# Decode step with sliding attention and a gated layer: the first two loads made one

## The chip, the cores and the metric

The kernel runs on one core of a Trainium2 chip. The metric is the device time of one execution in microseconds. TensorE (PE in the profile, its weight loads PEld), VectorE (DVE), ScalarE (ACT), GpSimd (POOL) and SyncE (SP) run side by side and wait for one another through semaphores. Sixteen DMA engines carry what SyncE issues; every load of this kernel is issued by SyncE.

## The reference

One token of two sequences (`B = 2`, `D = 512`) goes through a layer norm, and then through an attention over the last 2048 places of a cache and a gated layer, whose results are added to the input:

```python
xn = _layernorm(x, axis=-1)
return x + _A_ref(xn, A_k_cache, A_v_cache, A_wq, A_wo) + _B_ref(xn, B_w_gate, B_w_up, B_w_down)

# attention, 32 heads of 128
q = (x @ wq).reshape(B, Sq, Hq, Dh).transpose(0, 2, 1, 3)
k = k_cache[:, :, Sk - W:, :]; v = v_cache[:, :, Sk - W:, :]      # W = 2048
scores = einsum("bhqd,bhkd->bhqk", q, k) * (Dh ** -0.5)
o = einsum("bhqk,bhkd->bhqd", softmax(scores), v)
return o.transpose(0, 2, 1, 3).reshape(B, Sq, Hq * Dh) @ wo

# gated layer, F = 1376
return ((x @ w_gate) * (x @ w_up)) @ w_down
```

All is float32. The keys, values and weights are read once, some 159 MB.

## The kernel before

**One stream in order of use.** The host lays out the keys, values and weights of all heads as one long array, `stream`. The function `blocks()` lists what follows what: blocks, each a list of fields (kind, number, columns). A block is one DMA: 128 rows, one for each partition, and each row is contiguous in memory. A key block of a head is 4096 columns (two sequences, 16 places in each partition, 128 numbers), a value block as much; a quarter of the query weights (`wq`) or of the output weights (`wo`) for a head is 512.

**Tiles and the pump.** A step tile has 13,824 columns (55,296 bytes in each partition), and there are three (`BUFS = 3`). `pump()` walks through the blocks, takes a step tile when a new step begins, and issues the load on SyncE; it stops when three step tiles are held. `done(kind, i)` is called when the program has issued the last reader of a field; with the last field of a tile, the tile is given back and `pump()` goes on. On the chip the load into a reused tile then waits, on SyncE's queue, until the readers of the old contents are through. SyncE issues strictly in this order.

The very first block has a tile of its own, `first`, which is never given back: the input `x` as 8 columns, three small matrices of ones and zeros (`pick`, 16 columns; `rows`, 6; `carry`, 9), and the first quarter of the query weights of head group 0 (`w` 0, 512 columns). Together 551 columns, 275.5 KB. The first step tile then takes `w` 1 (1536 columns), and the keys with `wq` of heads 0 and 1, 5376 KB. The second has the first half of gate and up weights and head 2's keys (6400 KB); the third, the second half, head 3's keys, head 0's values and some of the down weights (6720 KB). From there each step takes three units of key or value, 6912 KB.

**What is done with them.** The layer norm reads `x`: a sum on VectorE, a matmul with a matrix of 1/512 that adds over the partitions, a subtraction, the same again for the squares, a square root on ScalarE, a reciprocal, and a copy that spreads the result to 128 columns (`xnb`). `project_first(0)` multiplies it with `w` 0 to give head 0's query on all partitions, `project_first(1)` with `w` 1 those of heads 1 to 3. For each head VectorE multiplies the keys with the query in place (`products`) and adds up rows of 128 (`sums`); GpSimd takes the maximum over the partitions, ScalarE the exponentials; TensorE weighs the values (`weigh`), `transpose` turns the result with the help of `pick`, and `project_o` adds its product with `wo` to `acc`. Values follow their head's keys by three heads (`LAG`). After head 3's sums comes the gate of the gated layer, whose transposes use `rows`. Near the end `acc` is copied out and goes into a wider form by a matmul with `carry`. The original rows of `x`, in `x_nat`, are added last.

**What sets the order.** TensorE, VectorE, ScalarE and SyncE run their instructions in the order in which the program is written: the wrapper `InOrder` ties each to the one before it, and all their instructions carry its line, L97 in the profile. Tiles are therefore told apart by name.

Of the kernel before, what the change touches and what calls it, by code (L numbers as in the profile page):

```python
# [8 lines left out]
F32 = mybir.dt.float32  # L9
# [7 lines left out]
P = 128  # L17
B, D, H, DH, SK, F = 2, 512, 32, 128, 8192, 1376
W = min(4096, max(256, SK // 4))
J = W // P  # L20
NC = D // P
FB = 4 * P
NFB = -(-F // FB)
# [4 lines left out]
RB = 8  # L28
M = RB * (B - 1) + 1
# [4 lines left out]
CK, CQ, CO = B * J * DH, NC * GC, D  # L34
CP = CQ // NC
UNIT = CK + max(CP, CO)
STEP = 3 * UNIT
# [6 lines left out]
def blocks():  # L44

    def wd(n):
        return [("wd", i, D) for i in range(*WD[n])]

    def k(h):
        return [("k", h, CK)] + ([("wq", h, CP)] if h + HG < H else [])

    def v(h):
        return [("v", h, CK), ("wo", h, CO)]  # L60

    def gu(half):
        n = NC * (FH[half][1] - FH[half][0])
        return [("wg", half, n), ("wu", half, n)]

    units = []
    for h in range(LAG, H - 1):
        units += [k(h), v(h - LAG)]
    ones = [("pick", 0, 8 * B), ("rows", 0, NFB * B), ("carry", 0, M)]
    first = [("x", 0, B * NC)] + ones + [("w", 0, NC * DH)]  # L70
    loads = [[("w", 1, CQ - NC * DH)] + k(0) + k(1), gu(0) + k(2)]
    loads += [gu(1) + units[0] + units[1] + wd(0) + [("wr", 0, NS * P)]]
    loads += [sum(units[i : i + 3], []) for i in range(2, len(units), 3)]
    loads += [k(H - 1) + v(H - 1 - LAG) + wd(1)]
    out = [(("f", 0), first)] + [(("s", i), fields) for i, fields in enumerate(loads)]
    late, last = ("s", len(loads)), ("s", len(loads) + 1)
    out += [(late, v(H - 3)), (late, v(H - 2)), (last, [("v0", H - 1, CL)])]
    out += [(last, [("v1", H - 1, CK - CL)]), (last, [("wo", H - 1, CO)] + wd(2))]
    return out + [(last, wd(n)) for n in range(3, len(WD))]
# [33 lines left out]
def kernel(  # L113
    ctx: ExitStack,
    tc: tile.TileContext,
    x_rows: bass.AP,
    stream: bass.AP,
    out: bass.AP,
):
    nc = tc.nc  # L120
    pe, dve, act, sp = (InOrder(tc, e) for e in (nc.tensor, nc.vector, nc.scalar, nc.sync))
    SCALE = float(DH) ** -0.5
    BUFS = 3

    const = ctx.enter_context(tc.tile_pool(name="const", bufs=1))
    steps = ctx.enter_context(tc.tile_pool(name="steps", bufs=BUFS))
# [6 lines left out]
    for key, fields in blocks():  # L133
        todo.append((key, fields, at))
        at += P * sum(w for _, _, w in fields)
    tiles, used, left, got = {}, {}, {}, {}
    held = 0
# [3 lines left out]
    def pump():  # L141
        nonlocal held
        while todo:
            key, fields, at = todo[0]
            if key not in tiles:
                if key[0] == "f":
                    n = sum(w for _, _, w in fields)
                    tiles[key] = const.tile([P, n], F32, name="first")
                elif held == BUFS:
                    return  # L150
                else:
                    held += 1
                    tiles[key] = steps.tile([P, STEP], F32, name="step")
                used[key] = 0
            todo.pop(0)
            c0 = used[key]
            for kind, i, w in fields:
                got[kind, i] = (tiles[key][:, used[key] : used[key] + w], key)
                used[key] += w
            c1 = used[key]  # L160
            src = stream[at : at + P * (c1 - c0)].rearrange("(p i) -> p i", p=P)
            sp.dma_start(tiles[key][:, c0:c1], src)

    def done(kind, i):
        nonlocal held
        _, key = got.pop((kind, i))
        left[key] -= 1
        if left[key] == 0 and key[0] != "f":
            del tiles[key]
            held -= 1  # L170
            pump()

    pump()
    xT = got["x", 0][0].rearrange("p (b c) -> p b c", b=B)
    pick = got["pick", 0][0].rearrange("p (r s b) -> p r s b", s=2, b=B)
    rows, carry = got["rows", 0][0], got["carry", 0][0][:M]

    x_nat = const.tile([P, P], F32, name="x_nat")
    dve.memset(x_nat, 0.0)
    sp.dma_start(x_nat[::RB, :], x_rows)  # L180

    mean_w = const.tile([P, P], F32, name="mean_w")
    dve.memset(mean_w, 1.0 / D)
# [30 lines left out]
        xc, xT, tr[:, 0:B].unsqueeze(2).to_broadcast([P, B, NC]), op=ALU.subtract  # L214
    )
    dve.tensor_tensor(sq, xc, xc, op=ALU.mult)
    dve.tensor_reduce(st[:, 1, :], sq, axis=AX.X, op=ALU.add)
    pe.matmul(tr[:, 8 : 8 + B], mean_w, st[:, 1, :], start=True, stop=True)
    act.activation(st[:, 2, :], tr[:, 8 : 8 + B], AF.Sqrt, bias=eps_t)
# [20 lines left out]
    def project_first(i):  # L240
        w = got["w", i][0].rearrange("p (c n) -> p c n", c=NC)
        if i == 0:
            q = q_first
        else:
            q_ps[0] = ps_q.tile([P, B, GC], F32, name="q")
            q = q_ps[0][:, :, DH:]
        for b in range(B):
            for c in range(NC):
                pe.matmul(
                    q[:, b, :], xnb[:, c * B + b, :], w[:, c, :],  # L250
                    start=(c == 0), stop=(c == NC - 1),
                )
        done("w", i)
# [26 lines left out]
    def sums(h):  # L280
        s_t[h] = small.tile([P, B, J], F32, name="s")
        dve.tensor_reduce(s_t[h], k_of(h), axis=AX.X, op=ALU.add)
        done("k", h)
# [164 lines left out]
    for _, fields in blocks():  # L448
        ks = [i for kind, i, _ in fields if kind == "k"]
        vs = [i for kind, i, _ in fields if kind == "v"]  # L450
        if vs and vs[-1] >= H - 5:
            break
        for n, h in enumerate(ks):
            products(h)
            project_q(h)
            if 2 <= h <= 3:
                project_gu(h - 2)
            sums(h)
            if h == LAG:
                gate()  # L460
            if vs and n == 0:
                values(vs)
            if h == LAG:
                down(0)
                down_rest()
            maxima(h)
            weights(h)
            if h >= 1:
                reciprocals(h - 1)
# [52 lines left out]
def laid_out(x):  # L522

    import numpy as np

    a = x["A_x"].reshape(B, D)
    first = {
        kind: np.zeros((P, w), a.dtype) for kind, _, w in blocks()[0][1][:4]
    }
    first["x"][:] = a.reshape(B, P, NC).transpose(1, 0, 2).reshape(P, B * NC)  # L530
    for b in range(B):
        for r in range(4):
            for s in range(2):
                first["pick"][8 * s + 4 * b + r :: 32, (2 * r + s) * B + b] = 1.0
        for n in range(NFB):
            first["rows"][32 * n + b, n * B + b] = 1.0
        first["carry"][RB * b, RB * b] = 1.0
    cache = {
        kind: x[name][:, :, SK - W :, :].reshape(B, H, P, J * DH).transpose(1, 2, 0, 3)
        for kind, name in (("k", "A_k_cache"), ("v", "A_v_cache"))  # L540
    }
    wq = x["A_wq"].reshape(P, NC, H // HG, GC).transpose(2, 0, 1, 3)
    wo = x["A_wo"].reshape(H, P, D)
    gu = {
        kind: x[name].reshape(P, NC, F)
        for kind, name in (("wg", "B_w_gate"), ("wu", "B_w_up"))
    }
    wd = x["B_w_down"]
    rest = wd[NFC * P :].reshape(FR, NS + 1, P)

    def field(kind, i):
        if kind in first:
            return first[kind]
        if kind in ("k", "v"):
            return cache[kind][i].reshape(P, CK)
        if kind in ("v0", "v1"):
            v = cache["v"][i].reshape(P, CK)
            return v[:, CL:] if kind == "v1" else v[:, :CL]
        if kind == "w":
            return (wq[0][:, :, DH:] if i else wq[0][:, :, :DH]).reshape(P, -1)  # L560
        if kind == "wq":
            return wq[i // HG + 1][:, i % HG, :]
        if kind == "wo":
            return wo[i]
        if kind == "wr":
            last = rest[:, NS, :].reshape(NS, FX, P).swapaxes(0, 1)
            return np.concatenate([rest[:, :NS, :], last]).reshape(P, NS * P)
        if kind == "wd":
            return wd[i * P : (i + 1) * P]
        return gu[kind][:, :, FH[i][0] : FH[i][1]].reshape(P, -1)  # L570

    parts = [
        np.concatenate([field(kind, i) for kind, i, _ in fields], axis=1).ravel()
        for _, fields in blocks()
    ]
    x_rows = np.zeros((D // P, 32 // RB, P), a.dtype)
    x_rows[:, :B] = a.reshape(B, D // P, P).transpose(1, 0, 2)
    return {
        "x_rows": x_rows.reshape(-1, P),
        "stream": np.concatenate(parts),  # L580
    }

# [31 lines left out]
```

## Time and profile before

| | |
|---|---|
| runs, median (lowest to highest) | 377.33 us (377.32 to 377.37), 3 runs |
| the profiled execution | 377.5 us |
| its span, first to last instruction | 375.7 us |
| HBM read | 159.48 MB |
| DMA issues on SyncE | 32, of them 30 into `first` and the step tiles |
| TensorE's granted clock, mean | 0.805 |

The span leaves out what lies before the first and after the last instruction, here 1.8 us. In the lines of the profile `step<-in_stream_dram` is a load into a step tile, `first<-in_stream_dram` the load of the first tile; SPq is SyncE's queue of issues. A number in brackets behind a line of the timeline is the idle time of that engine before it, and what ended it. The view of DMA issues gives the time from the issue of a load until its last byte has landed.

### The profile page before, as it was taken

The numbers are of one execution on the slowest core, as the hardware profiler recorded it, in microseconds if no ns is written. First come the engines' busy times: TensorE is split into PE (matmuls) and PEld (weight loads), VectorE is DVE, ScalarE is ACT, GpSimd is POOL, SyncE is SP. The second block draws the span as 40 slices with busy tenths as digits, with TensorE's granted clock in tenths as the row PEclk, the third lists the DMA queues.
The fourth block names the chain that finished last, engine by engine and source line by source line (L and its number), as shares of the span: only waits on it lengthen the run. The fifth ranks groups of instructions, "written<-read, shape, count | busy, mean of one in ns | idle before, by whom it ended". The sixth has DMA issues, their size and how long they took to land.

```text
span 375.7 us, 2858 instructions
## 1 busy us (share of the span) xinstructions
PE 254.2 (68%) x1084; PEld 88.5 (24%) x1084; DVE 294.1 (78%) x146; ACT 58.6 (16%) x259; POOL 25.3 (7%) x78
## 2 busy tenths in 40 slices
PE   3496497886547486854858476685846669637996
PEld 3241023331112122211212121231212122212334
DVE  3299691998599499769949976994996799599950
ACT  1021001122021111201112020211202011211131
POOL 1001000000000000100000100000000000000010
PEclk9998967998697666888768696885869676857999
DMA  8999999899999999999999999999999999999995
GB/s 346 445 436 454 426 408 471 383 465 449 395 466 406 442 455 400 459 418 436 460 400 449 424 430 459 402 442 430 430 459 406 437 444 436 419 431 443 398 421 221
DMA packets 4492, 159.70 MB, mean 425 GB/s; under 512 B 512, under 2 KB 640, under 8 KB 1152
## 3 DMA queue, kind: packets, MB, share of 16 engines
q1 hardware_dynamic: 4480, 159.54, 98.5%
q8 instruction: 8, 0.13, 0.1%
q14 instruction: 4, 0.03, 0.0%
HBM read 159.48 MB, written 0.06 MB: 425 GB/s over the span
## 4 chain that ended last, share of the span: by engine, by line
DMA 63%; DVE 26%; PE 8%; ACT 1%; issue 0%; SPq 0%; DVEq 0%
DMA step<-in_stream_dram 63%; DVE s L97 13%; DVE step L97 13%; PE o_ps L97 3%; PE q L97 2%; PE acc L97 2%; PE tr L97 1%; ACT o_sb L97 0%; DVE m L97 0%; ACT oT L97 0%; SPq L97 0%; DVE rec L97 0%; DVE o_out L97 0%; DVEq L97 0%
## 5 line engine op out<-in xcount | busy, mean ns | idle before, releaser
L97 DVE TENSOR_TENSOR step<-step,q 128x4096 f32<-128x4096 f32 x31 | 136.6, 4407 | 52.4 <-DMA step<-in_stream_dram 52.4
L97 PE MATMUL q<-step,xnb 128*128 128x512 f32 (+1 forms) x128 | 92.4, 872 | 76.4 <-DMA step<-in_stream_dram 76.4
L97 DVE TENSOR_REDUCE s<-step 128x32 f32<-128x4096 f32 x32 | 141.4, 4419 | 1.1
L97 PE MATMUL o_ps<-step,p 128*16 128x512 f32 x512 | 68.9, 672 | 11.5 <-DMA step<-in_stream_dram 11.5
L97 PEld LDWEIGHTS q<-step,xnb 128*128 128x128 f32 x128 | 32.3, 275 | 130.5 <-DMA step<-in_stream_dram 77.5
L97 PE MATMUL acc<-step,oT 128*9 128x512 f32 (+1 forms) x88 | 35.4, 552 | 9.3 <-ACT oT L97 8.1
L97 PE MATMUL tr<-first,o_sb 128*128 128x2 f32 (+2 forms) x198 | 28.1, 261 | 15.4 <-ACT o_sb L97 13.0
L97 ACT COPY o_sb<-o_ps 128x512 f32<-128x512 f32 (+1 forms) x25 | 14.1, 568 | 140.7 <-PE o_ps L97 140.7
L97 PEld LDWEIGHTS tr<-first,o_sb 128*128 128x128 f32 x198 | 26.0, 200 | 36.8 <-ACT o_sb L97 32.4
L290 POOL PARTITION_ALL_REDUCE mm<-m x32 | 11.3, 354 | 283.1 <-DVE rec L97 180.1
L97 PEld LDWEIGHTS o_ps<-step,p 128*16 128x16 f32 x512 | 13.4, 104 | 69.9 <-issue 54.4
L97 ACT ACTIVATE nm<-mm 128x2 f32<-128x2 f32 x32 | 6.5, 203 | 131.4 <-POOL mm L290 131.4
L97 ACT ACTIVATE p<-s,nm 128x16 f32<-128x16 f32 x64 | 19.2, 300 | 1.0
L97 ACT ACTIVATE oT<-tr,rec 128x1 f32<-128x1 f32 x64 | 12.2, 260 | 28.5 <-PE tr L97 28.5
L306 POOL PARTITION_ALL_REDUCE sum<-rs x32 | 12.7, 398 | 55.0 <-ACT p L97 55.0
L97 PE MATMUL o_ps<-step,xn 128*2 128x512 f32 (+1 forms) x48 | 13.9, 616 | 0.0
L97 ACT ACTIVATION_READ_ACCUMULATOR p<-s,nm 128x1 f32 x64 | 12.0, 187 | 0.0
L97 DVE TENSOR_TENSOR step<-step,tr 128x4096 f32<-128x4096 f32 x1 | 4.4, 4422 | 9.3 <-DMA step<-in_stream_dram 9.3
L97 PEld LDWEIGHTS acc<-step,oT 128*9 128x9 f32 x88 | 4.5, 91 | 19.4 <-ACT oT L97 12.7
L97 PE MATMUL q<-xnb,mean_w 128*128 128x512 f32 (+2 forms) x18 | 8.3, 551 | 0.0
L97 DVE TENSOR_TENSOR o_out<-acc,x_nat 128x128 f32<-128x128 f32 x1 | 0.3, 292 | 8.8 <-PE acc L97 8.8
L97 DVE TENSOR_REDUCE m<-s 128x2 f32<-128x32 f32 x32 | 5.9, 186 | 1.1
(39 smaller groups left out, 40.5 us busy)
## 6 DMA issues: line engine op xcount, KB each, us to landing
step<-in_stream_dram SPq DMA_DIRECT2D x16, 6912.0 KB, 31.1
step<-in_stream_dram SPq DMA_DIRECT2D x2, 6400.0 KB, 32.8
step<-in_stream_dram SPq DMA_DIRECT2D x1, 6720.0 KB, 45.4
step<-in_stream_dram SPq DMA_DIRECT2D x1, 6656.0 KB, 29.0
step<-in_stream_dram SPq DMA_DIRECT2D x1, 5376.0 KB, 15.3
step<-in_stream_dram SPq DMA_DIRECT2D x1, 4864.0 KB, 29.6
step<-in_stream_dram SPq DMA_DIRECT2D x2, 2304.0 KB, 17.1
step<-in_stream_dram SPq DMA_DIRECT2D x1, 1536.0 KB, 14.6
```

Source lines behind the costliest of these rows:

```text
L97: made = call(*args, **kwargs)
L290: nc.gpsimd.partition_all_reduce(mm, m, P, bass_isa.ReduceOp.max)
L306: nc.gpsimd.partition_all_reduce(sum_t[h], rs, P, bass_isa.ReduceOp.add)
```

## The change

The first block loses its tile. `x`, `pick` and `rows` become the first fields of the first step tile, followed by all of `w`, and the whole is one load of 11,294 columns (45,176 bytes a row). Since a step tile is given back, `pick` and `rows`, which are needed later, are copied by ScalarE into tiles of their own as soon as the load has landed; `x` is given up after the subtraction. `carry` leaves the stream and becomes an input of its own, 9 x 9, loaded by a DMA that SyncE issues behind that of `x_nat`. The constant tiles become 2048 bytes smaller in each partition, and all later tiles move down by as much. In the program built from it, ScalarE has one more load of its function table, between the two copies and the square root.

```diff
-    ones = [("pick", 0, 8 * B), ("rows", 0, NFB * B), ("carry", 0, M)]
-    first = [("x", 0, B * NC)] + ones + [("w", 0, NC * DH)]
-    loads = [[("w", 1, CQ - NC * DH)] + k(0) + k(1), gu(0) + k(2)]
+    first = [("x", 0, B * NC), ("pick", 0, 8 * B), ("rows", 0, NFB * B)]
+    loads = [first + [("w", 0, NC * DH), ("w", 1, CQ - NC * DH)] + k(0) + k(1), gu(0) + k(2)]
...
-    out = [(("f", 0), first)] + [(("s", i), fields) for i, fields in enumerate(loads)]
+    out = [(("s", i), fields) for i, fields in enumerate(loads)]
...
             if key not in tiles:
-                if key[0] == "f":
-                    n = sum(w for _, _, w in fields)
-                    tiles[key] = const.tile([P, n], F32, name="first")
-                elif held == BUFS:
+                if held == BUFS:
                     return
-                else:
-                    held += 1
-                    tiles[key] = steps.tile([P, STEP], F32, name="step")
+                held += 1
+                tiles[key] = steps.tile([P, STEP], F32, name="step")
...
-        if left[key] == 0 and key[0] != "f":
+        if left[key] == 0:
...
-    pick = got["pick", 0][0].rearrange("p (r s b) -> p r s b", s=2, b=B)
-    rows, carry = got["rows", 0][0], got["carry", 0][0][:M]
+    pick_t = const.tile([P, 8 * B], F32, name="pick")
+    act.copy(pick_t, got["pick", 0][0])
+    done("pick", 0)
+    pick = pick_t.rearrange("p (r s b) -> p r s b", s=2, b=B)
+    rows = const.tile([P, NFB * B], F32, name="rows")
+    act.copy(rows, got["rows", 0][0])
+    done("rows", 0)
...
+    carry = const.tile([M, M], F32, name="carry")
+    sp.dma_start(carry, carry_rows)
...
     dve.tensor_tensor(sq, xc, xc, op=ALU.mult)
+    done("x", 0)
```

The rest of the difference passes the new input through and fills it on the host's side, as before.

More of the change, by code (lines that the diff above doesn't have):

```diff
@@ L116 @@
     x_rows: bass.AP,
+    carry_rows: bass.AP,
     stream: bass.AP,
@@ L527, in laid_out @@
     first = {
-        kind: np.zeros((P, w), a.dtype) for kind, _, w in blocks()[0][1][:4]
+        kind: np.zeros((P, w), a.dtype) for kind, _, w in blocks()[0][1][:3]
     }
+    carry = np.zeros((M, M), a.dtype)
     first["x"][:] = a.reshape(B, P, NC).transpose(1, 0, 2).reshape(P, B * NC)
@@ L536, in laid_out @@
             first["rows"][32 * n + b, n * B + b] = 1.0
-        first["carry"][RB * b, RB * b] = 1.0
+        carry[RB * b, RB * b] = 1.0
     cache = {
@@ L579, in laid_out @@
         "x_rows": x_rows.reshape(-1, P),
+        "carry": carry,
         "stream": np.concatenate(parts),
```

## The prediction

> **What bounds the kernel now.** First the page: the busy shares, the queues, the chain that ended last.
>
> ```profile
> PE 254.2 (68%) x1084; PEld 88.5 (24%) x1084; DVE 294.1 (78%) x146; ACT 58.6 (16%) x259; POOL 25.3 (7%) x78
> ...
> q1 hardware_dynamic: 4480, 159.54, 98.5%
> q8 instruction: 8, 0.13, 0.1%
> ...
> DMA 63%; DVE 26%; PE 8%; ACT 1%; issue 0%; SPq 0%; DVEq 0%
> ```
>
> The DMA engines are busy 98.5% of the span; VectorE, the fullest engine, 78%. The chain puts 26% on VectorE. Read alone, that says that a later VectorE makes a later end. The reader has to check this against the transfers, because the chain stops at the instruction that released a load's issue, whether or not the queue was empty by then. So next: when each load is issued (SyncE's timeline, four windows), and how long it takes to land (the DMA view, the windows at 43 and 72 us).
>
> ```profile
> 0.72 0.38 SPq L97 DMA_DIRECT2D first<-in_stream_dram  x1
> 1.16 1.37 SPq L97 DMA_DIRECT2D step<-in_stream_dram  x3
> 34.54 0.33 SPq L97 DMA_DIRECT2D step<-in_stream_dram  x1
> 43.58 0.33 SPq L97 DMA_DIRECT2D step<-in_stream_dram  x1
> 72.90 0.33 SPq L97 DMA_DIRECT2D step<-in_stream_dram  x1
> ...
> step<-in_stream_dram SPq DMA_DIRECT2D x1, 6912.0 KB, 37.9
> ...
> step<-in_stream_dram SPq DMA_DIRECT2D x1, 6912.0 KB, 24.9
> ```
>
> Call the loads into step tiles s0, s1, s2 (issued one after the other from 1.16 us), s3 (34.54), s4 (43.58), s5 (72.90). s4 lands at 43.58 + 37.9 = 81.5, s5 at 72.90 + 24.9 = 97.8: 16.3 us apart for 6912 KB (7.08 MB), 434 GB/s. s5 was issued 8.6 us before s4 had landed. Who waited for the early landings (timeline), and the chain at both ends of the program:
>
> ```profile
> 16.58 4.42 DVE L97 TENSOR_TENSOR step<-step,tr 128x4096 f32<-128x4096 f32 x1 [9.33 <-DMA step<-in_stream_dram]
> 31.62 2.65 PE L97 MATMUL q<-step,xnb 128*128 128x512 f32 x4 [3.26 <-DMA step<-in_stream_dram]
> 47.48 4.42 DVE L97 TENSOR_TENSOR step<-step,q 128x4096 f32<-128x4096 f32 x1 [3.67 <-DMA step<-in_stream_dram]
> 65.25 4.42 DVE L97 TENSOR_TENSOR step<-step,q 128x4096 f32<-128x4096 f32 x1 [7.16 <-DMA step<-in_stream_dram]
> ...
> 1.16 15.32 DMA step<-in_stream_dram
> ...
> 34.54 30.69 DMA step<-in_stream_dram
> ...
> 343.55 19.66 DMA step<-in_stream_dram
> 363.21 0.04 issue
> ...
> DVE step L97 <- DMA step<-in_stream_dram: 61.7, 11, 9.3
> ```
>
> s0 lands at 16.48, s1 at 31.6, s2 at 47.5, s3 at 65.23. s3, issued at 34.54, had s2 still 12.9 us from landing. In every case the next load stood in the queue before the one ahead was through, and VectorE waited 61.7 us in all for data. The queue sets the end; the chain's VectorE pieces at the front are work that the queue covers. They count only if a load's issue becomes so late that the queue empties.
>
> **The change, part by part.**
>
> *One load for two.* Load "first" (275.5 KB: x, ones, first quarter of the first head group's weights) and s0 (5376 KB) become one of 11,294 columns, 45,176 bytes a row. The 9 columns of carry leave, 128 x 36 = 4.6 KB, 0.01 us at 434 GB/s. The bytes are otherwise the same, so what can be gained is start-up.
>
> ```profile
> first<-in_stream_dram SPq DMA_DIRECT2D x1, 275.5 KB, 2.9
> ...
> 0.50:1.50 1.00, 0.00 (x0) 0.00 (x0) 0.58 (x4) 0.78 (x1) 0.78 (x6) 1.00 0.00 0
> 1.50:2.00 0.50, 0.00 (x0) 0.00 (x0) 0.44 (x2) 0.50 (x1) 0.28 (x5) 1.00 0.67 62
> ```
>
> In the table of stretches (last columns: DMA share, GB/s) the transfers begin between 1.5 and 2.0 us, so 0.8 to 1.3 us after the issue at 0.72. 5.787 MB at 434 GB/s take 13.3 us; s0 landed at 16.48. 16.48 - 13.3 - (1.5 to 2.0) = 1.2 to 1.7 us are lost on start-up and landing. From 3.6 (0.72 + 2.9, first's landing) to 16.48 the 5.505 MB of s0 took 12.9 us against 12.7 at the steady rate, so nearly all of the loss lies in the first 3 us, and a single load has a first 3 us too. Bounds: 0 to -1.2 us; I take -0.3, nearer to zero because the loss stands with whichever load is first. The merged load then lands at about 16.2 to 16.4.
>
> In the Trainium skill, "DMA: Bandwidth & Descriptors", section "Anatomy of one DMA", a DMA costs about 2.0 us fixed plus its bytes. By that, one load fewer would give 375.3. The trace speaks against adding it up: from s0's landing to s1's 6.55 MB took 15.1 us, 434 GB/s, with no room for a fixed cost between queued loads.
>
> *The layer norm starts when all of it has landed.* The rows of its chain:
>
> ```profile
> 3.62 0.16 DVE L97 TENSOR_REDUCE st<-first 128x2 f32<-128x8 f32 x1 [0.82 <-DMA first<-in_stream_dram]
> ...
> 5.71 0.26 ACT L97 ACTIVATE st<-tr,eps_t 128x2 f32<-128x2 f32 x1 [3.71 <-PE tr L97]
> ...
> 7.20 3.75 PE L97 MATMUL tr<-first,xnb 128*128 128x128 f32 x16 [1.53 <-issue]
> ...
> 16.52 11.84 PE L97 MATMUL q<-step,xnb 128*128 128x384 f32 x24 [5.57 <-DMA step<-in_stream_dram]
> ```
>
> From 3.62 to the first head's query at 7.20 + 3.75 = 10.95 are 7.33 us. Today they lie beside s0's transfer, and VectorE then idles 9.33 us until 16.58. After the change they start at about 16.35, so head 0's products start near 23.7, 7.1 to 7.3 us later; I use 7.2. The two memsets of hT and hX stand on VectorE between and stay under TensorE's 3.75 us.
>
> The other edits on this chain: two ScalarE copies (128x16 and 128x6) wait for the same landing, ahead of the square root. Nearest rows:
>
> ```profile
> L97 ACT ACT_TABLE_LOAD x2 | 2.6, 1283 | 0.7 <-PEq L595 0.7
> ...
> L97 ACT COPY hT<-tr 128x6 f32<-128x6 f32 x4 | 0.7, 166 | 4.5 <-PE tr L97 4.5
> ```
>
> 2 x 0.17 = 0.34 us. The order of instructions in the changed program also has a second table load between the copies and the square root: 1.28. Together 1.62 us against 5.71 - 3.62 = 2.09 us that TensorE and VectorE need before the root can start: hidden, 0.4 us to spare. Without that cover it would be 1.6 us on the chain. The skill ("ScalarE: Activation LUTs", "What ACT_TABLE_LOAD costs") adds a drain of 1.38 us to each load; with it the root would come 0.9 us late.
>
> *What the 7.2 us do to the queue.* The step tile of s0 is free after head 1's sums, today 34.54, then 41.7. s3's packets must be there when the first DMA engine is through with s2. Stretches of half a microsecond show that:
>
> ```profile
> 46.00:46.50 0.50, 0.00 (x0) 0.00 (x0) 0.00 (x0) 0.00 (x0) 0.00 (x0) 0.96 0.00 0
> 46.50:47.00 0.50, 0.00 (x0) 0.00 (x0) 0.00 (x0) 0.00 (x0) 0.00 (x0) 0.50 3.13 1340
> ...
> 78.50:79.00 0.50, 0.02 (x1) 0.05 (x2) 0.47 (x2) 0.47 (x4) 0.00 (x0) 1.00 0.00 0
> 79.00:79.50 0.50, 0.50 (x2) 0.07 (x2) 0.50 (x1) 0.50 (x4) 0.00 (x0) 1.00 2.05 885
> ```
>
> Packets are booked where they start: s3's from 46.5, s5's from 79.0. Less the 1.3 us of start-up, the last harmless issue is 45.2 for s3 and 77.7 for s5. s3 at 41.7: 3.5 us to spare. Head 2 follows without a gap, so s4 is issued at 43.58 + 7.2 = 50.8, where s3's landing is 14 us off. TensorE: its 11.84 us block starts after the layer norm, ends near 35.5 instead of 28.4; the blocks for heads 2 and 3 move, but the one that s2 feeds still waits for 47.5. VectorE: head 3's products at 50.9 instead of 47.48, its two passes (8.85 us) end at 59.8, and the gate's product, today at 57.23, starts at 59.8:
>
> ```profile
> 57.23 0.69 DVE L97 TENSOR_TENSOR o_sb<-o_sb,o_ps 128x512 f32<-128x512 f32 x1 [0.87 <-PE o_ps L97]
> ...
> 62.78 3.61 PE L97 MATMUL o_ps<-step,p 128*16 128x512 f32 x16
> ...
> 72.06 0.82 PE L97 MATMUL acc<-step,hX 32*9 32x128 f32 x6
> ```
>
> The gate's transposes, head 0's values and the down projection follow it one by one until s2's tile is free at 72.9; 2.6 us later makes 75.5, 2.2 us inside the limit. Head 4 is free to start at s3's landing as before (VectorE done with the gate at 60.7), so all is in step again by 65 us on VectorE and by s5's landing, 97.8, on TensorE. On the end: 0, bounds 0 and, were the whole 7.2 us to reach s5's issue (80.1), 2.4.
>
> *The carrying matrix by itself.* One more DMA on SyncE's queue, 9 rows of 36 bytes behind x_nat, needed only by the matmuls near 357 us. Its issue (0.4 us) stands ahead of nothing: SyncE's next is s3 at 41.7. x_nat, issued 2.57, landed 45.1 later, 0.2 us behind s2:
>
> ```profile
> x_nat<-in_x_rows_dram SPq DMA_DIRECT2D x1, 8.0 KB, 45.1
> ```
>
> Bounds 0 to 0.2; I take 0.05.
>
> *Reload of s0's tile also waits for ScalarE's copies:* done 24 us earlier, 0.
>
> Sum: -0.3 + 0.05 + 0 = -0.25. The profiled execution took 377.5 us (span 375.7): 377.25. The median of the runs is 377.33, 0.17 lower: 377.1.
>
> **The rivals.**
>
> Slower: s5 is issued later than 77.7 and the queue runs dry there. For it: only 2.2 us to spare, and the granted clock in that stretch is uneven (0.50 in the rows at 46.5), so TensorE's part may move by more than VectorE does. Against: the slack of 0.87 us before the gate is counted already. From an issue at about 78.7 it passes +0.75 us net; with the full 7.2 us, 377.1 + 2.4 = 379.5. Chance 13%.
>
> Faster: the first load's start-up goes wholly, -1.2: 376.2; with the skill's fixed cost, 375.3. For it: 1.2 to 1.7 us are lost there. Against: a first load remains. Over half of it is needed to pass 0.75 us. Chance 8%.
>
> The chain's reading holds and VectorE's lateness reaches the end: 377.3 + 7.2 = 384.5. For it: 26% of the chain. Against: the 61.7 us of waiting for data and the next load always queued. Chance 3%.
>
> Forecast, the queue never empties: 377.1, own range 376.6 to 377.6. Chance 76%.
>
> **How the numbers follow.** 0.2% is 0.75 us (376.6 to 378.1), about what a measurement of this kernel can tell from no change. Same: 76%. Faster 8%. Slower 13 + 3 = 16%. The range takes the forecast's own, and the slower rival up to a gap of 1.3 us: 376.6 to 378.4.
>
> **What would show it.** Right: head 0's products near 23.7; the load after the first three issued near 41.7, the one into s2's tile near 75.5; landings from s3 on at 65 and then every 16.3 us; DMA share again 98 to 99%. Wrong: a stretch without packets near 47 or 80; the first landing not near 16.3 but a microsecond off; the square root starting much more than 2.1 us after the first reduction; a last load that lands more than 0.75 us from today's place.

## The result, and the profile after

The changed kernel takes 380.17 us (median of 6 runs, 379.48 to 380.76), the kernel before 377.35 (377.32 to 377.76): a ratio of 1.0069, 95% interval 1.0059 to 1.0080, so 2.8 us slower. Its runs spread over 1.3 us, those of before over 0.4. The profiled execution took 380.32 us, 2.8 more than that of before; its span is 378.5.

The page first: busy shares, the queue, the chain.

```profile
PE 253.4 (67%) x1084; PEld 88.6 (23%) x1084; DVE 294.1 (78%) x146; ACT 60.2 (16%) x262; POOL 25.3 (7%) x78
...
q1 hardware_dynamic: 4354, 159.53, 98.0%
...
DMA 54%; DVE 23%; PE 18%; issue 2%; ACT 2%; SPq 0%; DVEq 0%
```

VectorE's work is the same to a tenth of a microsecond. The queue's share fell from 98.5% to 98.0%, and the chain now has 18% on TensorE instead of 8%. Where the DMA engines stood still is seen in the table of stretches (last three columns: granted clock of TensorE, DMA share, GB/s), and the issues on both sides of the hole in SyncE's timeline and the DMA view (windows at 51 and 80 us):

```profile
72.00:76.00 4.00, 3.41 (x5) 0.67 (x6) 3.96 (x4) 1.20 (x7) 0.75 (x2) 0.50 1.02 442
76.00:80.00 4.00, 4.00 (x12) 1.04 (x11) 3.97 (x2) 0.00 (x0) 0.00 (x0) 0.65 0.54 235
...
51.20 0.33 SPq L96 DMA_DIRECT2D step<-in_stream_dram  x1
79.93 0.33 SPq L96 DMA_DIRECT2D step<-in_stream_dram  x1
...
step<-in_stream_dram SPq DMA_DIRECT2D x1, 6912.0 KB, 30.1
...
step<-in_stream_dram SPq DMA_DIRECT2D x1, 6912.0 KB, 20.2
```

s4, issued at 51.20, lands at 51.2 + 30.1 = 81.3; s5, issued at 79.93, lands at 100.1, 18.8 us later. Two queued loads of this size land 16.3 apart, so 2.5 us are lost here. Part of that is the stop, part the start after it: in the trace, s5's first packet on each DMA engine took 2.5 to 3.0 us, where packets of this size take 2.04 in the median. In the kernel before, 76 to 80 us has a DMA share of 1.02. The chain at both ends of the program, and the layer norm:

```profile
0.72 16.08 DMA step<-in_stream_dram
...
345.60 20.48 DMA step<-in_stream_dram
...
16.82 0.16 DVE L96 TENSOR_REDUCE st<-step 128x2 f32<-128x8 f32 x1 [14.02 <-DMA step<-in_stream_dram]
18.90 0.26 ACT L96 ACTIVATE st<-tr,eps_t 128x2 f32<-128x2 f32 x1 [0.48 <-PE tr L96]
...
24.18 4.42 DVE L96 TENSOR_TENSOR step<-step,tr 128x4096 f32<-128x4096 f32 x1 [3.74 <-PE tr L96]
```

The merged load lands at 16.80, s0 landed at 16.48. These 0.3 us do not last: s4 lands at 81.3, and landed at 81.5 before. s5 lands 2.3 us later than before (100.1 against 97.8), so 2.3 of the 2.8 us have come about by then, through the hole. The rest is added near the end: the load issued at 345.60 takes 20.48 us to land, the same load before, issued at 343.55, takes 19.66. Why is not shown. What made s5's issue late is TensorE's chain from the gate to the release of s2's tile:

```profile
60.84 0.39 PE L96 MATMUL tr<-rows,o_sb 128*128 128x6 f32 x2 [4.42 <-DVE o_sb L96]
...
66.03 3.61 PE L96 MATMUL o_ps<-step,p 128*16 128x512 f32 x16
70.34 1.87 PE L96 MATMUL tr<-pick,o_sb 128*128 128x2 f32 x8 [0.71 <-ACT o_sb L96]
...
74.46 4.69 PE L96 MATMUL acc<-step,hT 128*9 128x512 f32 x6
...
79.08 0.82 PE L96 MATMUL acc<-step,hX 32*9 32x128 f32 x6
```

It starts 2.9 us later than before and ends 7.0 later. For the same instructions the kernel before has these:

```profile
57.97 0.39 PE L97 MATMUL tr<-first,o_sb 128*128 128x6 f32 x2 [0.85 <-DVE o_sb L97]
67.09 1.05 PE L97 MATMUL tr<-first,o_sb 128*128 128x2 f32 x8 [0.70 <-ACT o_sb L97]
...
69.60 2.53 PE L97 MATMUL acc<-step,hT 128*9 128x512 f32 x6
```

1.87 against 1.05 and 4.69 against 2.53: the same matmuls at little more than half the pace. Stretches over the whole chain, from its first transpose to s5's issue, before and after (TensorE's busy time second, its granted clock third from the end):

```profile
57.97:72.90 14.93, 12.11 (x53) 5.38 (x53) 7.73 (x4) 2.91 (x15) 0.75 (x2) 0.77 0.96 415
...
60.84:79.93 19.09, 16.28 (x53) 6.88 (x53) 14.93 (x8) 2.91 (x15) 1.11 (x3) 0.55 0.96 417
```

The same 53 matmuls keep TensorE busy 16.28 us instead of 12.11, at a granted clock of 0.55 instead of 0.77. That is the 4.2 us by which the chain is longer.

### The profile page after: what moved, and what is told of

Read it like the earlier page. It is cut to its first block, busy times and chain, and to the rows that moved or that the text cites. A ratio compares the mean times of both kernels' runs of the same rounds, so it can differ in the third digit from the quotient of the medians.

```text
span 378.5 us, 2861 instructions
## 1 busy us (share of the span) xinstructions
PE 253.4 (67%) x1084; PEld 88.6 (23%) x1084; DVE 294.1 (78%) x146; ACT 60.2 (16%) x262; POOL 25.3 (7%) x78
## 4 chain that ended last, share of the span: by engine, by line
DMA 54%; DVE 23%; PE 18%; issue 2%; ACT 2%; SPq 0%; DVEq 0%
DMA step<-in_stream_dram 54%; DVE step L96 12%; DVE s L96 11%; PE o_ps L96 5%; PE acc L96 5%; PE tr L96 4%; PE q L96 4%; ACT o_sb L96 1%; ACT oT L96 1%; DVE m L96 0%; ACT hT L96 0%; DVE o_sb L96 0%; SPq L96 0%; DVE rec L96 0%; DVE st L96 0%
## 5 line engine op out<-in xcount | busy, mean ns | idle before, releaser
L96 PE MATMUL q<-step,xnb 128*128 128x512 f32 (+1 forms) x128 | 87.5, 830 | 64.1 <-DMA step<-in_stream_dram 64.1
L96 PE MATMUL o_ps<-step,p 128*16 128x512 f32 x512 | 70.4, 685 | 10.7 <-DMA step<-in_stream_dram 10.7
L96 PEld LDWEIGHTS q<-step,xnb 128*128 128x128 f32 x128 | 30.8, 263 | 116.2 <-DMA step<-in_stream_dram 61.0
L96 PE MATMUL acc<-step,oT 128*9 128x512 f32 (+1 forms) x88 | 36.9, 571 | 9.3 <-ACT oT L96 8.1
L96 ACT COPY o_sb<-o_ps 128x512 f32<-128x512 f32 (+1 forms) x25 | 14.1, 568 | 136.0 <-PE o_ps L96 136.0
L96 PE MATMUL tr<-pick,o_sb 128*128 128x2 f32 (+1 forms) x184 | 25.6, 261 | 13.0 <-ACT o_sb L96 13.0
L96 PEld LDWEIGHTS tr<-pick,o_sb 128*128 128x128 f32 x184 | 24.1, 203 | 33.5 <-ACT o_sb L96 32.5
L295 POOL PARTITION_ALL_REDUCE mm<-m x32 | 11.4, 357 | 276.6 <-DVE rec L96 170.4
L96 PE MATMUL tr<-st,mean_w 128*128 128x2 f32 x4 | 1.2, 363 | 17.7 <-DVE st L96 17.7
L96 PE MATMUL o_ps<-step,xn 128*2 128x512 f32 (+1 forms) x48 | 11.9, 548 | 0.0
L96 DVE RECIPROCAL rec<-sum 128x2 f32<-128x2 f32 x32 | 5.0, 155 | 6.0 <-POOL sum L311 6.0
L96 PE MATMUL acc<-step,hT 128*9 128x128 f32 (+2 forms) x58 | 8.4, 366 | 0.0
```

Source lines behind the costliest of these rows:

```text
L96: made = call(*args, **kwargs)
L295: nc.gpsimd.partition_all_reduce(mm, m, P, bass_isa.ReduceOp.max)
```

## The experiments

The theory: the queue empties at s5, because VectorE's lateness reaches the gate and TensorE's chain behind it runs slower too. Rivals: the transfers themselves (45 KB rows, small rows of carry), the copies and the table load, the place of the tiles.

### The merged load split again

```diff
-    loads = [first + [("w", 0, NC * DH), ("w", 1, CQ - NC * DH)] + k(0) + k(1), gu(0) + k(2)]
+    loads = [[("w", 1, CQ - NC * DH)] + k(0) + k(1), gu(0) + k(2)]
-    out = [(("s", i), fields) for i, fields in enumerate(loads)]
+    out = [(("s", 0), first + [("w", 0, NC * DH)])]
+    out += [(("s", i), fields) for i, fields in enumerate(loads)]
```

> The changed kernel, with its first load issued in two again: x, pick, rows and the first quarter of the weights, then the rest, both into the first step tile. Copies, second table load and the carrying matrix's own DMA stay. Theory (the layer norm starts 13 us late, so the load into the third tile is issued at 79.9 us, after the queue has emptied, and the hole of 2.5 us stays to the end): the layer norm starts near 3.6 us again, that load is issued near 73 us, and the time is 377.3 to 377.5. Rival (the copies, the table load, the 36-byte rows or the other place of the tiles cost it): the time stays near 380.2. Rival (the merged load's own start, landing 0.3 us later, and nothing more): 379.9.

377.50 us (377.36 to 377.74); ratio to before 1.0003, interval 0.9994 to 1.0013. s5 was issued here:

```profile
73.60 0.33 SPq L97 DMA_DIRECT2D step<-in_stream_dram  x1
```

The whole loss is in the merging. The copies, the second table load, the 36-byte rows of carry and the other place of the tiles cost nothing that can be measured.

### The last wait taken away

```diff
-                down(0)
-                down_rest()
+                for c in range(*WD[0]):
+                    done("wd", c)
+                done("wr", 0)
```

> The changed kernel, leaving out the first part of the down projection and its rest (the matmuls that are the last to read the third tile): part of the gated layer is not computed. TensorE's 6.6 us between project_o of head 0 and the release go. Theory (the queue runs empty because that tile comes free too late): the issue comes near 74.5 us, no hole, 377.5 to 377.8, what is left over 377.35 being the 0.3 us by which the merged load landed later. Rival (the loss is in the transfers themselves: rows of 45 KB that start unaligned, small rows of the carrying matrix): near 380.

377.59 us (377.48 to 377.84), ratio 1.0001 (0.9991 to 1.0010); s5 issued at 74.72. The load is still merged, the layer norm still 13 us late, and the loss is gone when s2's tile comes free in time. So the transfers as such are not what costs.

### The late layer norm alone

x moved from the first load of the kernel before to the end of its second.

```diff
-    first = [("x", 0, B * NC)] + ones + [("w", 0, NC * DH)]
-    loads = [[("w", 1, CQ - NC * DH)] + k(0) + k(1), gu(0) + k(2)]
+    first = ones + [("w", 0, NC * DH)]
+    loads = [[("w", 1, CQ - NC * DH)] + k(0) + k(1) + [("x", 0, B * NC)], gu(0) + k(2)]
...
     dve.tensor_tensor(sq, xc, xc, op=ALU.mult)
+    done("x", 0)
```

> The kernel before, with one thing changed: x's 8 columns come at the end of the second load instead of in the first. Two loads, carry in the stream, no copies. Theory (only the layer norm's late start matters): the load into the third tile is issued near 79 to 80 us, landings 18 to 19 us apart there, time 379.4 to 380.3, with runs that spread by about a microsecond as the changed kernel's do. Rival (merging the load, the copies or the carrying matrix cost it): 377.4.

380.71 us (380.13 to 380.85): a time near the theory's, but not by its path, and so a miss. s5 was issued at 77.73, at the limit, not at 79 to 80, and landed 16.3 us after s4, as queued loads do, so the profile shows next to no hole. The step tiles had moved 32 bytes down with the smaller first tile, and their packets took longer everywhere (2.045 us in the median instead of 2.041). That place is worth 1.2 us by a run below; the rest of the 3.3 us is not accounted for. So the move was made again with the place kept:

```diff
-    first = ones + [("w", 0, NC * DH)]
+    first = ones + [("pad", 0, B * NC), ("w", 0, NC * DH)]
```

> The same as the run before it with x at the end of the second load, but with 8 unused columns in the first load where x was, so that the step tiles stay where they are in the kernel before (in that run they stood 32 bytes lower, and its packets of 55,296 bytes took 2.045 us in the median instead of 2.041). Theory (the late layer norm alone makes the loss): the load into the third tile is issued at 77 to 80 us, the landing after it comes 17 to 19 us after the one ahead, time 379.0 to 380.7. Rival (in the run before it, the place of the tiles made the loss, and lateness alone costs nothing): 377.4 to 377.7.

379.44 us (378.46 to 380.40), ratio 1.0054 (1.0036 to 1.0072). Lateness alone, with two loads, no copies and carry in the stream, makes some 2.0 of the 2.8 us; what makes the rest is not shown. The profiled execution, the fastest of its five at 378.46, issued s5 at 77.94. The stretches from 76 to 82 us (clock, DMA share, GB/s last) in the kernel before, the changed kernel and this one:

```profile
76.00:82.00 6.00, 4.70 (x23) 2.14 (x16) 5.97 (x2) 1.78 (x8) 0.40 (x1) 1.00 1.02 442
```

```profile
76.00:82.00 6.00, 6.00 (x19) 1.67 (x21) 5.97 (x2) 0.00 (x0) 0.00 (x0) 0.77 0.82 304
```

```profile
76.00:82.00 6.00, 5.66 (x29) 1.58 (x27) 5.97 (x2) 0.27 (x1) 0.00 (x0) 0.94 1.02 415
```

(442 - 304) GB/s over 6 us are 0.83 MB, 1.9 us of transfer at 434 GB/s, in the changed kernel; 0.16 MB, 0.4 us, in this execution. That is the stop alone. The slow first packets behind it add, as a mean over the sixteen engines, 0.7 us in the changed kernel and 0.3 here. In the profiles whose queue stayed full no packet of that size between 77 and 83 us takes more than 2.3.

### The place of the step tiles

The kernel before with 32 unused bytes a partition ahead of its step tiles.

```diff
+    shift = const.tile([P, 8], F32, name="shift")
+    nc.gpsimd.memset(shift, 0.0)
     eps_t = const.tile([P, 1], F32, name="eps_t")
```

> The kernel before with an unused tile of 32 bytes a partition among the constants, so that all step tiles begin 32 bytes higher. Nothing else changes. If a tile's place makes its packets slower, by the 0.05 us per load seen with the tiles 32 bytes lower, 22 large loads give 1.1 us: 378.4. If it doesn't: 377.4.

378.62 us (378.39 to 378.96), ratio 1.0032 (1.0020 to 1.0043): 1.2 us for nothing but the address. The changed kernel's tiles moved by 2048 bytes, and in the first experiment that place cost nothing.

### The gate ahead of head 3's sums

```diff
-            sums(h)
             if h == LAG:
                 gate()
+            sums(h)
```

> The changed kernel with the gate put ahead of head 3's sums instead of behind them: VectorE does the gate's product (0.7 us) between its two passes over head 3, so TensorE's chain to the release of the third tile starts about 3.6 us sooner, and all the work stays. Theory (the hole is there because VectorE reaches the gate late and TensorE's chain behind it ends after 77.7 us): the issue comes at 75 to 77 us, no hole, 377.5 to 377.8. Rival (it is TensorE's clock alone, which falls in any case): the issue is at 78 us or later and the time at 379 or above.

377.55 us (377.40 to 377.75), ratio 1.0000 (0.9991 to 1.0009). All work is done, the load is merged, and only VectorE's order differs. s5's issue and the gate's product:

```profile
74.79 0.33 SPq L96 DMA_DIRECT2D step<-in_stream_dram  x1
...
57.25 0.69 DVE L96 TENSOR_TENSOR o_sb<-o_sb,o_ps 128x512 f32<-128x512 f32 x1 [1.44 <-PE o_ps L96]
```

The product stands at 57.25, where the kernel before has it (57.23), the issue comes 5.1 us sooner than in the changed kernel, and the hole is closed. TensorE's clock fell here too: the chain took 16.8 us, at 0.70, and ended in time because it began 2.9 us sooner. So a clock of 0.70 does not make the loss by itself.

### A smaller first load

x, pick, rows, w and head 0's keys in the first load, head 1's keys in a second one into the same tile.

```diff
-    loads = [first + [("w", 0, NC * DH), ("w", 1, CQ - NC * DH)] + k(0) + k(1), gu(0) + k(2)]
+    loads = [k(1), gu(0) + k(2)]
-    out = [(("s", i), fields) for i, fields in enumerate(loads)]
+    out = [(("s", 0), first + [("w", 0, NC * DH), ("w", 1, CQ - NC * DH)] + k(0))]
+    out += [(("s", i), fields) for i, fields in enumerate(loads)]
```

> The changed kernel with a smaller first load: x, pick, rows, all of the first weights and head 0's keys (rows of 26.7 KB, 3.4 MB), then head 1's keys as a second load into the same tile. Theory: the first load lands near 9.7 us, the layer norm ends near 17.0, where the kernel before starts head 0 at 16.6, so VectorE is late by half a microsecond, the issue into the third tile is near 73 to 74 us, no hole, 377.4 to 377.7. Rival (the merging itself, not how late it lands, makes the loss): 379 or above.

377.90 us (377.44 to 377.98), ratio 1.0007 (0.9998 to 1.0017). The first load landed at 11.4, not 9.7 (why was not settled); head 0's products began at 18.80, s5 was issued at 73.28, and the time is 0.2 us above the range expected. A merged load is harmless while it lands soon.

### TensorE's granted clock

Extra matmuls of 128 columns into unused columns, first 14 ahead of the gate's transposes and one behind each, then 18 ahead of them and none behind.

```diff
+    def fill(n):
+        for _ in range(n):
+            pe.matmul(tr[:, 3 * P :], mean_w, spare_in[:, 0:P], start=True, stop=True)
...
         dve.tensor_tensor(h_sb, g_sb, gu_ps[1], op=ALU.mult)
+        fill(18)
```

> The changed kernel with 21 more matmuls of 128 columns around the gate's transposes (14 ahead of them, one behind each), which write to unused columns: more work on TensorE, no gap of 4.4 us in it while it waits for VectorE. Theory (of the 7.0 us that the issue into the third tile came later, 2.9 are VectorE's and 4 are TensorE at a granted clock of 0.50 from 62 to 79 us, after that gap): the granted clock stays near 1.00 there, the issue comes at 75 to 77 us, the hole closes, 377.5 to 378.0. Rival (the chain of late steps alone, whatever the clock): the issue stays at 79 us or later, and 380 or above.

380.38 us (379.37 to 381.59). A miss: the matmuls behind each transpose stretched the chain itself (a transpose every 0.87 us instead of 0.65), s5 was issued at 79.48, and the clock fell a little later all the same.

> The changed kernel with 18 more matmuls of 128 columns ahead of the gate's transposes and none behind them: TensorE's gap of 4.4 us while it waits for VectorE is filled, and the transposes keep their own pace. If the 17 us at a granted clock of 0.50 in the changed kernel (61.7 to 78.8 us) come from that gap: the low clock lasts about 7 us as in the kernel before (60.1 to 66.9), the issue into the third tile comes at 75.5 to 77.5 us, 377.6 to 378.5. If they don't (the light transposes alone do it, or the phase of the clock's windows): the issue stays at 78.5 us or later, 379 or above.

379.14 us, but from 377.56 to 380.98. The issue in the profile (75.20) came a little sooner than expected, and the median is a miss. By their spans, four of the ten runs stand at 375.6 to 375.8 us, where the queue loses nothing, the others at 376.8 to 379.0; three runs, the profiled one among them, have 2.9 to 3.3 us outside the span instead of 1.8 to 2.0. The second profiles of this kernel and of the changed kernel:

> The kernel with 18 matmuls in TensorE's gap once more, for a second profile, since its runs reach from 377.56 to 380.98 us. If the phase of the low clock decides: another low stretch between 55 and 78 us than in the first profile (69.9 to 73.3), another issue time than 75.2, and a span above 375.6 as far as the issue is later than 77.7. If not: the same issue near 75.2, whatever the span.

> The changed kernel unaltered, for a second profile. If the granted clock around the gate differs between executions of one program and sets the hole: the low stretch lies elsewhere than 61.7 to 78.8 us, the issue into the third tile moves with it between 76 and 80 us, and the span goes with the issue, 1 us for 1 us beyond 77.7. If the clock is the same each time: issue again near 79.9 and span 378.5.

The stretch of 57 to 74 us (granted clock third from the end) with s5's issue, in this order: the changed kernel's first and second profile, and the first and second profile with the 18 matmuls.

```profile
57.00:74.00 17.00, 10.35 (x40) 5.63 (x41) 12.88 (x7) 2.91 (x15) 0.75 (x2) 0.64 1.07 462
...
79.93 0.33 SPq L96 DMA_DIRECT2D step<-in_stream_dram  x1
```

```profile
57.00:74.00 17.00, 10.44 (x40) 5.97 (x41) 12.75 (x7) 2.91 (x15) 0.47 (x2) 0.54 1.02 442
...
80.15 0.33 SPq L96 DMA_DIRECT2D step<-in_stream_dram  x1
```

```profile
57.00:74.00 17.00, 14.19 (x82) 8.21 (x82) 12.79 (x8) 2.91 (x15) 0.75 (x2) 0.90 1.02 442
...
75.20 0.33 SPq L96 DMA_DIRECT2D step<-in_stream_dram  x1
```

```profile
57.00:74.00 17.00, 14.02 (x79) 7.63 (x79) 12.79 (x8) 2.91 (x15) 0.75 (x2) 0.90 1.04 452
...
74.79 0.33 SPq L96 DMA_DIRECT2D step<-in_stream_dram  x1
```

With the gap filled TensorE does more, its clock is 0.90 instead of 0.54 to 0.64, the chain ends 4.7 to 5.4 us sooner, and the spans are 375.6 and 376.0 us, against 378.5 and 378.2. So VectorE's lateness alone, at a good clock, brings the issue to about 75, as forecast. The timed runs of the filled kernel up to 380.98 have no profile; that the clock fell in them as well is likely and not shown. The second profiles differ less than was thought: the changed kernel's low stretch began at 58.4 us instead of 61.7, but its issue moved by 0.2 us and its span not with it; the filled kernel's moved from 69.9 to 65.1 us, and its issue by 0.4. So they do not explain why the runs of one kernel spread.

Across the profiles, the chain from the first transpose to s5's issue is longer the lower the clock over it: 14.1 and 14.2 us at 0.88 with the gap filled; 14.9 and 15.0 at 0.77 (before, smaller first load); 16.6 to 16.8 at 0.69 and 0.70 (split, 32 bytes, gate first); 17.1 and 17.4 at 0.66 and 0.63 (late x); 19.1 and 19.4 at 0.55 and 0.53 (the changed kernel twice). Without the filling, TensorE's wait at the gate grows in the same order, from 0.85 to 1.05 us in the second and third group to 3.6 and 4.1, and to 4.3 and 4.4. A long wait and a low clock go together. But the chain varies by 1.9 us even where nothing is late, nearly the forecast's whole margin, and what sets the length of a low stretch is not shown.

Over all profiles with the step tiles in their place, issue and span go together: up to 75.20 (72.90, 73.28, 73.60, 74.72, 74.79 twice, 75.20) the span is 375.6 to 376.1; at 77.94 it is 376.7, at 79.48 377.9, at 79.93 378.5, at 80.15 378.2.

## Why the prediction was wrong

**What bounds the kernel.** Right: the queue, and VectorE's 26% of the chain cost nothing as long as a load stood ready.

**The limit.** Right: 77.7 us was given as the last harmless issue of s5. The profiles put the knee between 75.20 and 77.94.

**The step that failed.** "2.6 us later makes 75.5, 2.2 us inside the limit." The 2.6 were 2.9. The mistake is that the chain behind the gate was carried over at the old durations, 14.9 us from the first transpose to the release; it took 19.1 (60.84 to 79.93), because TensorE ran at a granted clock of 0.55 instead of 0.77 over it. Of the 7.0 us by which s5's issue moved, 2.9 are VectorE's lateness and 4.2 the slower chain (rounded). The forecast had put TensorE's unevenness down as a chance in the slower rival. That rival is what happened, with its place, its limit and nearly its price: 2.2 us past the limit cost 2.5 us between the landings, for the 2.4 named there. It was given 13%.

What could have been read beforehand: the prediction quotes the clock of 0.50 at 46.5 us, but not the clock of the chain that it carries over, which the trace of the kernel before had at 0.77: full clock for part of it, 0.50 from 60.1 to 66.9 us. Durations like these are not fixed, and a matmul of the same shape takes up to 1.9 times as long at 0.50 (1.91 and 3.61 us for 16 of `weigh`'s). And late VectorE makes TensorE wait at the gate, 4.42 us instead of 0.85. In the Trainium skill, "TensorE: Matmul & The Clock Gate", section "Part 1: The HAM clock gate (the 'warmup' mystery)", an idle window of about 3.4 us halves the clock. By that rule a wait of 4.4 us had to be checked against 3.4, and the trace of the changed kernel agrees in one point: the clock fell to 0.50 at 61.7 us, 0.9 us behind the wait. It does not agree in another: the fall at 60.1 us in the kernel before has a wait of 0.85 us ahead of it.

**The first load's start.** The term was -0.3 and measured +0.3: landing at 16.80, 16.73 in the second profile, against 16.48. The bounds (0 to -1.2) excluded a loss without a reason for it. In the trace, the first packet of the merged load on each engine took 2.2 to 3.0 us, the median 1.67; in the kernel before the first packets are of 2204 bytes, and the longest took 0.68. As a mean over the engines, the two first loads before lose 0.6 us in slow packets, the merged one 0.8. The 0.3 us did not reach the end: the two kernels that keep the merged load and issue s5 by 74.8 us take 377.55 and 377.59. The fixed 2.0 us that the prediction quotes from the Trainium skill, "DMA: Bandwidth & Descriptors", is stated in its section "Anatomy of one DMA" for DMAs that GpSimd issues; all loads here are SyncE's.

**Copies, table load, carry.** Right, all hidden: the square root started 18.90 - 16.82 = 2.08 us after the first reduction, against 2.09 before, and the first experiment has their sum at 0.1 us, at most 0.5 by its interval. The drain of 1.38 us that the prediction weighs, by which the root would have come 0.9 us late, does not show.

**s3's issue.** Forecast 41.7, measured 42.2: right, and harmless.

## What to carry to other kernels

A queue that is always full hides late work only up to the issue that has the least time to spare; find that issue, and follow every engine on the way to it. When one engine is made late, the engine that waits for it may come back at a lower clock (here 0.55 instead of 0.77 over the chain), so durations copied from the old trace can be too short, and a margin of 2.2 us was not enough. Before a margin is trusted, the granted clock over the very stretch that is carried over should be read. If a load is merged for fewer issues, what the first steps need should still land first, or the work that frees the tightest tile should be moved ahead: one line of order (the gate ahead of the sums) took the whole loss away.

## What the runs showed of the hardware

Moving the step tiles by 32 bytes in each partition made the kernel before 1.2 us slower (378.62 against 377.44). That is some 6 to 7 ns on each of the about 180 large packets that one DMA engine carries (22 large loads, 8 rows each per engine; an estimate). A move by 2048 bytes cost nothing that could be measured (377.50 in the first experiment).

The first packets behind a stop of the queue were slow: 2.5 to 3.0 us for 55,296 bytes after the hole of the changed kernel, against a median of 2.04. So a queue that runs dry cost more than the time that it stood still: 1.9 us of stop, 2.5 us between the landings.

The low stretches of TensorE's clock are not the same from execution to execution of one program (0.64 and 0.54 over the same 17 us), and they lasted even while TensorE was busy 3.4 of 4 us (72 to 76 us in the changed kernel, at 0.50). Kernels whose issue stood near or past the limit had the wider spread: 1.3 us for the changed kernel, 1.9 with late x and 3.4 with the gap filled, against 0.4 to 0.6 for the altered kernels that issue in time, and up to 1.1 over 23 runs of the kernel before. That the clock makes this spread is likely and not shown.
